# Attention by thirds of the queries: score products and value products in clusters, one exponential over two PSUM banks

## The chip, the cores and the metric

The kernel runs on one core of one Trainium2 chip. The metric is the device time of one execution in microseconds (us). Every execution was checked against the reference, and all of them were correct. With one core, an execution is called "slow" when it is over 1.5% above the fastest of the same kernel, otherwise "fast".

Engine names in the profile: PE is TensorE's matrix products, PEld its weight loads, DVE is VectorE, ACT is ScalarE, POOL is GpSimd, SP or SPq is the queue from which the transfers (DMA) are issued. L419 is line 419 of the kernel shown. Line numbers differ between kernels. SBUF and PSUM are the two on-chip memories in which the kernel allocates its tiles; in this kernel every product of TensorE goes to a PSUM tile.

## The reference, cut to what matters

The reference is attention with cluster routing (a query sees only the keys of its own cluster), followed by a mixture of small experts. There are 4 batches, 8 heads, 768 positions and a head size of 64.

```python
q_assign = argmax(q_n @ c_n.T); k_assign = argmax(k_n @ c_n.T)   # 16 clusters a head
scores = where(q_assign == k_assign, scale * q @ k.T, -1e9)
attn = softmax(scores)                  # over 768 keys
x = attn @ v                            # (4, 8, 768, 64) -> rows of 512
# then: gate of 8 experts, best 2, x + sum of w * (x @ A[e]) @ B[e]
```

## The kernel before: the parts that matter

The 32 heads are taken in 16 pairs. Each pair passes through these stages, several pairs at a time:

- Transposes of q and k, and the routing: logits, argmax, one-hot rows. The one-hot rows enter the score product as 16 more rows, so that the mask costs no step of its own.
- Scores with the keys on the partitions, and their exponentials ET. VectorE sums the exponentials into SS.
- Denominators: a product with ones on TensorE, a copy d_sb, four small transfers that spread the sums over 128 partitions (d_pk), a reciprocal r_pk, a transfer to DRAM (r_dr), and a broadcast from DRAM to all partitions (rDb).
- Value products into o, and a multiplication `xT = o * rDb` on VectorE.

The last two stages are what the argument is about. This is how they look before the change:

```python
def denominators(p):
    ...                                             # ones-product into ps
    nc.scalar.copy(d_sb[:], ps[:])
    for j in range(4):
        nc.sync.dma_start(d_pk[32*j:32*j+32, :], d_sb[32*j:32*j+1, :])
    def second():                                   # put into the program 3.2 us later
        nc.vector.reciprocal(r_pk[:], d_pk[:])
        r_dr = drp.tile([2, S], F32, name="r_dr")   # DRAM
        nc.sync.dma_start(r_dr[:].rearrange("h (i e) -> (h i) e", e=12), r_pk[:])
        rb = wk.tile([128, S], F32, name="rDb")
        for h in range(2):                          # two transfers, one for each head
            nc.sync.dma_start(rb[64*h:64*h+64, :], r_dr[h:h+1, :].to_broadcast([64, S]))
        rDb[p] = rb
    W.later(3.2, second)

def pv(p, c, kc):                                   # c: 512 or 256 queries, kc: key chunk
    for h in range(2):
        nc.tensor.matmul(ps[64*h:64*h+64, :], v_nat[p][:, h, kc*D:(kc+1)*D],
                         src[:, h, kc, :], start=(kc == 0), stop=(kc == T - 1))
...
    nc.vector.tensor_tensor(xT[p][:, a:b], O[p, c][:], rDb[p][:, a:b], ALU.mult)
```

A small scheduler decides the order of the program. It places the 18 score units of the next pair, one by one, between the value products of this pair.

The softmax here doesn't subtract the row's maximum and nothing guards it: scores larger than these inputs give would overflow.

Of the kernel before, what the change touches and what calls it, by code (L numbers as in the profile page):

```python
# [22 lines left out]
class Weave:  # L23
# [3 lines left out]
    def __init__(self):  # L27
        self.clock = 0.0
        self.heap = []
        self.n = 0  # L30

    def later(self, dt, fn):
        heapq.heappush(self.heap, (self.clock + dt, self.n, fn))
        self.n += 1

    def step(self, cost, fn):
        fn()
        self.clock += cost
        self.due()

    def due(self):
        while self.heap and self.heap[0][0] <= self.clock:
            heapq.heappop(self.heap)[2]()

    def flush(self):
        while self.heap:
            t, _, fn = heapq.heappop(self.heap)
            self.clock = max(self.clock, t)
            fn()

    def phase(self, events, fill):

        t0 = self.clock
        events = sorted(events, key=lambda e: e[0])
        fill = list(fill)
        while events or fill:
            if events and (events[0][0] <= self.clock - t0 or not fill):
                _, cost, fn = events.pop(0)
            else:
                cost, fn = fill.pop(0)  # L60
            self.step(cost, fn)
# [3 lines left out]
def kernel(  # L65
# [22 lines left out]
    C0, C1 = 512, 256  # L88
# [6 lines left out]
    etp = ctx.enter_context(tc.tile_pool(name="etp", bufs=2))  # L95
    wk = ctx.enter_context(tc.tile_pool(name="wk", bufs=1))
    wk2 = ctx.enter_context(tc.tile_pool(name="wk2", bufs=2))
    xp = ctx.enter_context(tc.tile_pool(name="xp", bufs=7))
# [4 lines left out]
    psc = ctx.enter_context(tc.tile_pool(name="psc", bufs=4, space=bass.MemoryType.PSUM))  # L103
# [3 lines left out]
    W = Weave()  # L107
# [7 lines left out]
    def load_qk(p):  # L115
        b, h = bh(p)
        t = nat.tile([128, 2, T, 2, D], F32, name="qk_nat")
        for w, x in ((0, q), (1, k)):
            for i in range(2):
                nc.sync.dma_start(t[:, w, :, i, :], x[b, h + i].rearrange("(p t) d -> p t d", t=T))  # L120
        qk_nat[p] = t

# [5 lines left out]

    load_qk(0)
# [78 lines left out]


    qkT = {}  # L210

    def turn(p, g):
        if g == 0:
            qkT[p] = wk.tile([128, 2 * S], F32, name="qkT")
        ps = psm.tile([128, 4, 128], F32, tag="m")
        src = qk_nat[p]
        for i in range(4):
            n = 4 * g + i
            w, t = divmod(n, T)
            nc.tensor.transpose(ps[:, i, :], src[:, w, t].rearrange("p h d -> p (h d)"), ident_f[:])  # L220
        dst = qkT[p][:, g * 512:(g + 1) * 512]
        if g == 1:
            nc.scalar.copy(dst, ps[:].rearrange("p i c -> p (i c)"))  # L223
        else:
            nc.vector.tensor_copy(dst, ps[:].rearrange("p i c -> p (i c)"))  # L225

    def rounded(p):
        x = qkT[p]
        qd, kd = Q2[p % 2], K2[p % 2]
        nc.gpsimd.tensor_copy(qd[0:64, 0, :].bitcast(F32R), x[0:64, 0:S])  # L230
        nc.gpsimd.tensor_copy(kd[0:64, 0, :].bitcast(F32R), x[0:64, S:2 * S])
        nc.gpsimd.tensor_copy(qd[:, 1, :].bitcast(F32R), x[:, 0:S])
        nc.vector.tensor_copy(kd[64:128, 1, :].bitcast(F32R), x[64:128, S:2 * S])
# [4 lines left out]
    def route(p):  # L238
        j = p % NP
        ps = psm.tile([128, 384], F32, tag="m")  # L240
# [6 lines left out]
        rt = wk2.tile([128, 384], F32, name="rt_sb")  # L247
        nc.scalar.copy(rt[:], ps[:])  # L248
        rt_sb[p] = rt

    def turn_logits(p):
        ps = psm.tile([128, 24, 16], F32, tag="m")
        for m in range(3):
            nc.tensor.transpose(ps[:].rearrange("p g c -> p (g c)")[:, m * 128:(m + 1) * 128],
                                rt_sb[p][:, m * 128:(m + 1) * 128], ident_f[:])
        mx = wk2.tile([128, 24], F32, name="mx")
        nc.vector.tensor_reduce(mx[:], ps[:], axis=AX.X, op=ALU.max)
        nc.vector.tensor_tensor(oh[p % 2][:, :, 0:16], ps[:],  # L258
                                mx[:].unsqueeze(2).to_broadcast([128, 24, 16]), ALU.is_equal)

    def turn_onehot(p):
        ps = psm.tile([128, T, 128], BF16, tag="m")
        v_ = oh[p % 2][:].rearrange("p (t g) c -> p t (g c)", g=4)
        for t in range(T):
            nc.tensor.transpose(ps[:, t, :], v_[:, t], ident_b[:])  # L265
        ohs = wk.tile([128, S], F32, name="ohs")
        nc.scalar.activation(ohs[:], ps[:].rearrange("p t c -> p (t c)"), ACTF.Copy,  # L267
                             scale=mscale[:, 0:1])
        qd, kd = Q2[p % 2], K2[p % 2]
        nc.sync.dma_start(qd[64:80, 0, :], ohs[0:16, :])  # L270
        nc.sync.dma_start(kd[64:80, 0, :], ohs[64:80, :])
        nc.sync.dma_start(qd[0:16, 1, :], ohs[32:48, :])
        nc.sync.dma_start(kd[0:16, 1, :], ohs[96:112, :])


    ET0, ET1, SS = {}, {}, {}

    def score_unit(p, u):
        if u == 0:
            ET0[p] = etp.tile([128, 2, T, C0], F32, name="ET0")  # L280
            ET1[p] = etp.tile([128, 2, T, C1], F32, name="ET1")
            SS[p] = wk2.tile([128, 2, S], F32, name="SS")
        qd, kd = Q2[p % 2], K2[p % 2]
        ps = psc.tile([128, 512], F32, name="sc")
        h = u % 2
        rows = 80 if h == 0 else 128
        if u < 12:
            kc = u // 2
            nc.tensor.matmul(ps[:], kd[0:rows, h, kc * 128:(kc + 1) * 128].bitcast(F32R),  # L289
                             qd[0:rows, h, 0:C0].bitcast(F32R))  # L290
            dst = ET0[p][:, h, kc, :]
        else:
            k2 = (u - 12) // 2
            for i in range(2):
                kc = 2 * k2 + i
                nc.tensor.matmul(ps[:, i * C1:(i + 1) * C1],  # L296
                                 kd[0:rows, h, kc * 128:(kc + 1) * 128].bitcast(F32R),
                                 qd[0:rows, h, C0:S].bitcast(F32R))
            dst = ET1[p][:, h, 2 * k2:2 * k2 + 2, :].rearrange("p a c -> p (a c)")
        nc.scalar.activation(dst, ps[:], ACTF.Exp, bias=expbias[:], scale=SCALE)  # L300
        W.later(1.3, lambda: add_unit(p, u))

    def add_unit(p, u):
        h = u % 2
        if u < 12:
            kc = u // 2
            E0, acc = ET0[p], SS[p][:, h, 0:C0]
            if kc == 1:
                nc.vector.tensor_tensor(acc, E0[:, h, 0, :], E0[:, h, 1, :], ALU.add)
            elif kc > 1:  # L310
                nc.vector.tensor_tensor(acc, acc, E0[:, h, kc, :], ALU.add)  # L311
        else:
            k2 = (u - 12) // 2
            E1, acc = ET1[p], SS[p][:, h, C0:S]
            if k2 == 0:
                nc.vector.tensor_tensor(acc, E1[:, h, 0, :], E1[:, h, 1, :], ALU.add)
            else:
                for i in range(2):
                    nc.vector.tensor_tensor(acc, acc, E1[:, h, 2 * k2 + i, :], ALU.add)  # L319
# [4 lines left out]
    def denominators(p):  # L324
        ps = psm.tile([128, 384], F32, tag="m")
# [4 lines left out]
        d_sb = wk.tile([128, 384], F32, name="d_sb")  # L330
        nc.scalar.copy(d_sb[:], ps[:])  # L331
        d_pk = wk2.tile([128, 12], F32, name="d_pk")
        for j in range(4):
            nc.sync.dma_start(d_pk[32 * j:32 * j + 32, :], d_sb[32 * j:32 * j + 1, :])  # L334

        def second():
            r_pk = wk2.tile([128, 12], F32, name="r_pk")
            nc.vector.reciprocal(r_pk[:], d_pk[:])  # L338
            r_dr = drp.tile([2, S], F32, name="r_dr")
            nc.sync.dma_start(r_dr[:].rearrange("h (i e) -> (h i) e", e=12), r_pk[:])  # L340
            rb = wk.tile([128, S], F32, name="rDb")
            for h in range(2):
                nc.sync.dma_start(rb[64 * h:64 * h + 64, :], r_dr[h:h + 1, :].to_broadcast([64, S]))
            rDb[p] = rb
        W.later(3.2, second)


    O = {}
    xT, xTb = {}, {}

    def pv(p, c, kc):
        n = (C0, C1)[c]
        if kc == 0:
            O[p, c] = pso.tile([128, n], F32, name=f"o{c}")
        ps = O[p, c]
        src = (ET0, ET1)[c][p]
        for h in range(2):
            nc.tensor.matmul(ps[64 * h:64 * h + 64, :], v_nat[p][:, h, kc * D:(kc + 1) * D],
                             src[:, h, kc, :], start=(kc == 0), stop=(kc == T - 1))
        if kc == T - 1:  # L360
            W.later(0.9, lambda: pv_out(p, c))

    def pv_out(p, c):
        if p not in rDb:
            W.later(0.4, lambda: pv_out(p, c))
            return
        if c == 0:
            xT[p] = xp.tile([128, S], F32, name="xT")
            xTb[p] = xbp.tile([128, S], BF16, name="xTb")
        a, b = ((0, C0), (C0, S))[c]  # L370
        nc.vector.tensor_tensor(xT[p][:, a:b], O[p, c][:], rDb[p][:, a:b], ALU.mult)  # L371
        nc.gpsimd.tensor_copy(xTb[p][:, a:b], xT[p][:, a:b])  # L372
# [4 lines left out]
    def gate(b):  # L377
        ps = psm.tile([128, 256], F32, tag="m")
# [5 lines left out]
        gl = mo.tile([96, 256], F32, name="gl")  # L384
        nc.scalar.copy(gl[:], ps[0:96, :])
        ms["gl"] = gl
# [113 lines left out]
    for i in range(2):  # L500
        zpart(b, i)
# [32 lines left out]
```

## Time and profile before

| | before |
|---|---|
| median of 3 executions (us) | 405.53 (404.97 to 406.09) |
| span of the profiled execution (us) | 400.8 |
| TensorE busy, VectorE busy, ScalarE busy | 91%, 67%, 58% |
| mean granted TensorE clock | 0.972 |
| a pair of heads (us) | 21.4 |

The first fence is the page's part on busy time, and from its 40 slices of the span the rows for TensorE (tenths busy) and for the TensorE clock that was granted (tenths of full speed).

```profile
span 400.8 us, 5985 instructions
PE 364.4 (91%) x2026; PEld 163.5 (41%) x2041; DVE 270.3 (67%) x548; ACT 232.2 (58%) x375; POOL 70.7 (18%) x92
...
PE   5437999999999999999999999999999999999645
...
PEclk9959999999999999999999999999999999999958
```

TensorE is at "9" from the fifth slice to the thirty-seventh, with the clock at nine tenths or more: it is the bound, and its order of work sets the time. The next fence is the timeline of TensorE before, in the middle of the run (start, duration, engine, line, operation, names, shapes, count).

```profile
209.30 1.08 PE L358 MATMUL o_1865<-ET_1650,v_nat 128*64 128x512 f32 x4
210.31 0.50 PE L289 MATMUL sc<-Q_0_152,K_0_154 128*128 128x512 f32 x1
210.64 0.60 PE L220 MATMUL ps<-ident_f,qk_nat 128*128 128x128 f32 x4
```

A single score product (L289) stands between other kinds of work. The numbers 128\*64 and 128\*128 are the tile of the array that a product takes. Each excursion from value products to one score product and back costs about 0.36 us beyond what the products themselves stream, by their start times. For example, two groups of four value records start at 186.72 and 188.16 us with one score product between them; at the spacing of long runs (0.21 us for 256 columns of values, 0.118 us for 256 of scores, so twice that here for 512) they would take 2 x 0.42 + 0.24 = 1.08 of these 1.44 us. This is what the change wants to save.

Two more views of before follow. The first is the list of waits of VectorE (who waited for whom: us in total, times, longest us), the second the list of transfer issues (KB each, median us from issue to landing).

```profile
DVE xT L371 <- DMA rDb<-r_dr: 47.1, 12, 5.7
```

```profile
rDb<-r_dr SPq DMA_DIRECT2D x32, 192.0 KB, 3.3
```

VectorE waits 47 us in total for the reciprocals' broadcast, while TensorE's own list of waits shows it waiting for the multiplication only once, for 5.5 us.

### The profile page before, as it was taken

Reading aid. Unit: us, or ns where it says so; the run is one execution under the profiler, and the core shown is the slowest. Engines: PE = TensorE matmul, PEld = TensorE weight load, DVE = VectorE, ACT = ScalarE, POOL = GpSimd, SP = SyncE. Lnnn points to the kernel's source line nnn. Section 1 sums busy time; section 2 is a strip of 40 time slices with the busy share of each in tenths; the row PEclk is TensorE's granted clock in tenths of the full one; section 3 lists DMA queues with packets and bytes.
Section 4 is the critical chain, followed back from the end, with each engine's and each line's share of the span. In section 5 each row is a group of like instructions: output and inputs, shape, how many; then the busy total and the mean of one; then the engine's idle time right before and its main releaser. Section 6 shows DMA issues by size and latency. Waiting matters only on the chain. (4 is left out here: it accounts for less than half of the span.)

```text
span 400.8 us, 5985 instructions
## 1 busy us (share of the span) xinstructions
PE 364.4 (91%) x2026; PEld 163.5 (41%) x2041; DVE 270.3 (67%) x548; ACT 232.2 (58%) x375; POOL 70.7 (18%) x92
## 2 busy tenths in 40 slices
PE   5437999999999999999999999999999999999645
PEld 2224343342424344454435353545443544433323
DVE  4237939668492979876586798875959797638043
ACT  1119766565646575757767676757676756663101
POOL 3202204012130401312131303030404030101000
PEclk9959999999999999999999999999999999999958
DMA  8726425160332416153626142363531211220204
GB/s 169 130 42 149 119 61 119 22 158 11 89 81 60 118 23 157 24 152 102 149 77 152 51 105 71 86 172 88 144 87 42 60 41 29 86 68 26 69 25 157
DMA packets 72974, 35.77 MB, mean 89 GB/s; under 512 B 62576, under 2 KB 66672, under 8 KB 72944
## 3 DMA queue, kind: packets, MB, share of 16 engines
q1 hardware_dynamic: 72944, 35.39, 35.4%
q8 instruction: 16, 0.26, 0.3%
q14 instruction: 14, 0.11, 0.1%
HBM read 25.74 MB, written 6.39 MB: 80 GB/s over the span
## 5 line engine op out<-in xcount | busy, mean ns | idle before, releaser
L372 POOL CAST xTb<-xT 128x512 bf16<-128x512 f32 (+1 forms) x32 | 23.9, 749 | 280.3 <-DVE xT L371 280.3
L289 PE MATMUL sc<-Q_0_152,K_0_154 80*128 80x512 f32 x96 | 43.4, 481 | 1.6 <-DMA K_0_154<-ohs 0.9
L289 PE MATMUL sc<-Q_1_153,K_1_155 80*128 80x512 f32 x96 | 42.1, 475 | 0.1
L220 PE MATMUL ps<-ident_f,qk_nat 128*128 128x128 f32 x192 | 31.6, 290 | 0.3
L289 PEld LDWEIGHTS sc<-Q_0_152,K_0_154 80*128 80x128 f32 x96 | 16.9, 188 | 32.2 <-issue 14.7
L220 PEld LDWEIGHTS ps<-ident_f,qk_nat 128*128 128x128 f32 x192 | 22.3, 146 | 18.2 <-DVE SS L311 4.9
L289 PEld LDWEIGHTS sc<-Q_1_153,K_1_155 80*128 80x128 f32 x96 | 16.7, 188 | 31.3 <-issue 18.2
L225 DVE COPY qkT<-ps 128x512 f32<-128x512 f32 x32 | 22.0, 687 | 7.1 <-PE ps L220 7.1
L329 PE MATMUL ps<-SS,ones 128*32 128x384 f32 x128 | 23.1, 498 | 3.3 <-DVE SS L319 2.6
L267 ACT ACTIVATE ohs<-ps,mscale 128x768 f32<-128x768 bf16 x16 | 14.4, 901 | 17.5 <-PE ps L265 17.5
L331 ACT COPY d_sb<-ps 128x384 f32<-128x384 f32 x16 | 7.7, 478 | 26.8 <-PE ps L329 18.1
L296 PE MATMUL sc<-Q_0_152,K_0_154 80*128 80x256 f32 (+1 forms) x96 | 22.2, 325 | 0.6 <-ACT ET_285 L300 0.6
L296 PE MATMUL sc<-Q_1_153,K_1_155 80*128 80x256 f32 (+1 forms) x96 | 21.9, 322 | 0.0
L338 DVE RECIPROCAL r_pk<-d_pk 128x12 f32<-128x12 f32 x16 | 3.7, 228 | 24.0 <-DMA d_pk<-d_sb 23.8
L296 PEld LDWEIGHTS sc<-Q_1_153,K_1_155 80*128 80x128 f32 (+1 forms) x96 | 13.9, 189 | 10.5 <-issue 4.6
L296 PEld LDWEIGHTS sc<-Q_0_152,K_0_154 80*128 80x128 f32 (+1 forms) x96 | 14.2, 189 | 9.7 <-issue 4.2
L223 ACT COPY qkT<-ps 128x512 f32<-128x512 f32 x16 | 9.4, 589 | 14.9 <-PE ps L220 12.9
L248 ACT COPY rt_sb<-ps 128x384 f32<-128x384 f32 x16 | 7.7, 479 | 16.9 <-PE ps L245 16.6
L245 PE MATMUL ps<-qkT,cnP 128*32 128x384 f32 x128 | 17.2, 498 | 0.2
L448 ACT COPY ot<-ps 128x512 f32<-128x512 f32 x12 | 7.0, 585 | 14.4 <-PE ps L444 8.2
L441 PE MATMUL ps<-ident_f,xT 128*128 128x128 f32 x96 | 14.9, 278 | 0.5 <-ACT ot L448 0.3
L265 PE MATMUL ps<-ident_b,oh_156 128*128 128x128 bf16 x48 | 4.4, 232 | 10.4 <-DVE oh_156 L258 10.4
(296 smaller groups left out, 790.3 us busy)
## 6 DMA issues: line engine op xcount, KB each, us to landing
qk_nat<-in_q_dram SPq DMA_DIRECT2D x32, 192.0 KB, 3.5
qk_nat<-in_k_dram SPq DMA_DIRECT2D x32, 192.0 KB, 4.1
v_nat<-in_v_dram SPq DMA_DIRECT2D x16, 384.0 KB, 4.3
rDb<-r_dr SPq DMA_DIRECT2D x32, 192.0 KB, 3.3
out_dram<-ot SPq DMA_DIRECT2D x24, 256.0 KB, 2.1
d_pk<-d_sb SPq DMA_DIRECT2D x64, 1.5 KB, 1.7
Q_0_152<-ohs SPq DMA_DIRECT2D x16, 48.0 KB, 2.1
K_0_154<-ohs SPq DMA_DIRECT2D x16, 48.0 KB, 2.1
```

Source lines behind the costliest of these rows:

```text
L220: nc.tensor.transpose(ps[:, i, :], src[:, w, t].rearrange("p h d -> p (h d)"), ident_f[:])
L223: nc.scalar.copy(dst, ps[:].rearrange("p i c -> p (i c)"))
L225: nc.vector.tensor_copy(dst, ps[:].rearrange("p i c -> p (i c)"))
L245: nc.tensor.matmul(ps[o:o + 32, :].rearrange("p (m c) -> p m c", m=3), cnP[:, j, :], xv[:, w, f])
L248: nc.scalar.copy(rt[:], ps[:])
L267: nc.scalar.activation(ohs[:], ps[:].rearrange("p t c -> p (t c)"), ACTF.Copy, scale=mscale[:, 0:1])
L289: nc.tensor.matmul(ps[:], kd[0:rows, h, kc * 128:(kc + 1) * 128].bitcast(F32R), qd[0:rows, h, 0:C0].bitcast(F32R))
L296: nc.tensor.matmul(ps[:, i * C1:(i + 1) * C1], kd[0:rows, h, kc * 128:(kc + 1) * 128].bitcast(F32R), qd[0:rows, h, C0:S].bitcast(F32R))
L329: nc.tensor.matmul(ps[o:o + 32, :], ones[:], SS[p][:, h, f * 384:(f + 1) * 384])
L331: nc.scalar.copy(d_sb[:], ps[:])
L372: nc.gpsimd.tensor_copy(xTb[p][:, a:b], xT[p][:, a:b])
L441: nc.tensor.matmul(ps[:, dc * 128:(dc + 1) * 128], xT[NP * b + dc][:, t * 128:(t + 1) * 128], ident_f[:], is_transpose=True, start=(dc == ...
```

## The change

The intent: take the queries of a pair in three thirds of 256. A slot for one third has eight score products of the next pair in a row, other work, four more score products, other work, and then the value products of this pair in a row (12 calls, which the trace shows as 24 records; below they are called 24 products). An exponential covers two PSUM banks (1,024 columns), so there are 9 a pair and not 18. A new scheduler keeps estimates of when each engine is done. The diff in its core, with cuts marked by `...`:

```diff
-    etp = ctx.enter_context(tc.tile_pool(name="etp", bufs=2))
+    etp = ctx.enter_context(tc.tile_pool(name="etp", bufs=4))
-    psc = ctx.enter_context(tc.tile_pool(name="psc", bufs=4, ... PSUM))
+    psc = ctx.enter_context(tc.tile_pool(name="psc", bufs=2, ... PSUM))   # two banks each
 ...
     def score_unit(p, t, u):
+        ps = psc.tile([128, 2, 2, TQ], F32, name="sc")
+        for i in range(2):
+            for h in range(2):
+                nc.tensor.matmul(ps[:, i, h, :], kd[...], qd[..., t*TQ:(t+1)*TQ])
+        W.op("ACT", 1.12, lambda: nc.scalar.activation(ET[p, t][:, 2*u:2*u+2]..., ps[:]..., ACTF.Exp, ...))
 ...                                 # adds over 1,024 columns: E0+E1, +E2, then the halves into SS
     def denominators(p):
 ...
-            for h in range(2):
-                nc.sync.dma_start(rb[64 * h:64 * h + 64, :], r_dr[h:h + 1, :].to_broadcast([64, S]))
-            rDb[p] = rb
+            def fill():
+                nc.sync.dma_start(rb[:], r_dr[:].unsqueeze(1).to_broadcast([2, 64, S]))
+                rDb[p] = rb
+            W.op("SP", 0.6, lambda: nc.sync.dma_start(r_dr[:]..., r_pk[:]),
+                 x, lag=1.6, then=lambda x: W.op("SP", 0.6, fill, x, key=("rDb", p), lag=3.4))
 ...
+    o4 = pso.tile([128, 4, TQ], F32)               # four thirds in two banks, one tile
     def pv(p, t):
+        i = NT * p + t
+        for kc in range(T):
             for h in range(2):
+                nc.tensor.matmul(o4[64 * h:64 * h + 64, i % 4, :], v_nat[p][...], ET[p, t][:, kc, h, :], ...)
 ...
+            nc.vector.tensor_tensor(xT[p][:, a:b], o4[:, i % 4], rDb[p][:, a:b], ALU.mult)
 ...
+    def slot(p, t):
+        if t == 0: ...; rounded(p + 2)             # three casts on GpSimd, one on VectorE
+        score_unit(p + 1, t, 0); score_unit(p + 1, t, 1)
+        for c in early: pe(*c)
+        score_unit(p + 1, t, 2)
+        for c in late: pe(*c)
+        pv(p, t)
```

Several transfers were also merged: q, k, and, in `fill`, the two broadcasts of the reciprocals into one.

## The prediction

> **What bounds the kernel now.** TensorE's order of work. The profile's first part gives TensorE 91% busy, VectorE 67%, ScalarE 58%; the slices show TensorE at "9" from about 50 to 365 us at full granted clock. Modelled ends hide gaps, so I read starts in the trace. A head pair takes 21.4 us (15 pairs between 42.6 us, the first value product, and 363 us, the last score product). Neighbours of a kind start 0.118 us (score products of 256 columns, also in a run of eight alternating heads) or 0.21 us apart (value products of 256). A round trip from values to one score product and back costs about 0.36 us beyond the streaming, and there are 218 runs of scores. The Trainium skill, "TensorEngine Tiling (Array Packing)", Key Properties, says that changing the tiling mode drains TensorE; values (128x64 tiles), denominators (128x32) and scores (full width) are different modes, and the 0.36 us agrees. Per pair, scores take 6.8 us and values 9.4 us.
>
> **What the change does**, per pair (three slots of eight score products, other work, four more, other work, 24 clustered value records):
> - Scores: 3 x (1.15 + 0.66) = 5.4 us, from runs of 8 and 4 in the trace.
> - Values: the one clustered group in the trace (pair 15, 256 columns) takes 2.69 us, so 8.0 us.
> - Other work unchanged: 3.5 us, and 1.6 us more with expert work.
> - Sum 16.9 us for four pairs, 18.5 us for eleven: 271 us instead of 320.
> - The third score unit waits for the first exponential: 1.12 us, extrapolated from 0.69 us at 512 columns with the copies' 0.85 ns a column. Costs 0.4 to 0.7 us a pair, 7 us.
> - ScalarE: 18 x 0.69 = 12.4 us becomes 9 x 1.12 = 10.1 us. Off the path.
> - VectorE: adds 3 x (1.20 + 1.20 + 0.68) = 9.2 us instead of about 11, but a 0.69 us copy more: 14.5 to 16 us of a pair of 17 to 19 us, nearly a second bound. It is in order, two PSUM buffers serve all other work, and the four value buffers share two banks, so the multiplication out of one half can hold up products into the other. I allow 0.8 us a pair, 12 us.
>
> Steady part about 290 us, 30 less. The start gets 2 us longer (one-hot rows come after two turns). The tail gets 6 us shorter: before, the last denominators wait behind adds and the reciprocals land 18.7 us after the last score product; that becomes about 13 us. In sum some 35 to 40 us less, nearly all of it on the critical path.
>
> **Predicted: 366 us, 8 in 10 between 353 and 382. Chances: faster by over 2% 0.96, within 2% 0.03, slower 0.01.**
>
> **What would show it.** Value clusters near 2.7 us, score clusters near 1.2 and 0.65 us; pairs of 17 to 20 us; TensorE with idle time before scores put down to ScalarE, before other work to VectorE; VectorE's share near 75%; ScalarE's busy time down by some 35 us; exponentials of 1.12 us; the last reciprocals some 13 us after the last score product.
>
> **What would make it wrong.** If VectorE, in order, is held by a late reciprocal transfer (it idled 47 us for these before, unharmed, by the list of waits), TensorE stops with it and the gain halves. If the multiplication and the products of one bank lock each other often, the same. If the schedule hides both, about 355 us.

## The result, and the profile after

The time went up. Ratios here and below are the mean time of one kernel's fast runs over that of the other's fast runs of the same rounds, so they are not quite the ratio of the medians quoted.

| | before | after |
|---|---|---|
| median (us) | 405.25 (4 executions, 404.36 to 406.09) | 506.53 (4 executions, 506.14 to 511.15) |
| ratio, 95% interval | | 1.2526 (1.2448 to 1.2603) |
| span of the profiled execution (us) | 400.8 | 504.5 |
| granted clock | 0.972 | 0.851 |
| a pair of heads (us) | 21.4 | 27.1 |

All these executions are fast. A pair of heads is the time from the first value product to the last score product, divided by 15, in both columns. Of the 104 us between the two spans, 85 us are lost between these two products, 8 us before them and 10 us after them. First the same parts of the page for after.

```profile
span 504.5 us, 6704 instructions
PE 360.3 (71%) x2617; PEld 229.9 (46%) x2617; DVE 267.6 (53%) x401; ACT 189.7 (38%) x218; POOL 92.1 (18%) x108
...
PE   6186939494958858397695939588595959875926
...
PEclk9679959697887978789797978879797988987978
```

TensorE now has holes: slices of 3 to 5 tenths stand beside slices of 9, and its clock falls to 7 tenths in slices among them. VectorE and ScalarE are less busy too, as a share. Nothing is saturated, so something makes everybody wait. The page's part on the chain of work that ended last names it (shares of the span, by engine and then by line; the second line is long, and is shown whole).

```profile
DMA 43%; PE 32%; DVE 11%; SPq 4%; ACT 4%; issue 3%; DVEq 0%; POOL 0%; ACTq 0%
DMA rDb<-r_dr 35%; PE o_183 L419 18%; PE sc L345 6%; DMA r_dr<-r_pk 4%; ACT ET L348 3%; DVE xT L431 2%; PE ps L381 2%; DMA d_pk<-d_sb 2%; SPq L392 1%; PE ps L258 1%; DVE mx L299 1%; DVE ACC L366 1%; PE ps L518 1%; DVE ACC L362 1%; DMA c_sb<-in_centroids_dram 1%
```

One transfer, the broadcast of the reciprocals, makes 35% of the chain. The lists of waits of after, first TensorE's longest, then VectorE's, say the same from the side of the engines.

```profile
PE o_183 L419 <- DVE xT L431: 96.7, 15, 8.6
```

```profile
DVE xT L431 <- DMA rDb<-r_dr: 95.1, 16, 9.4
```

Fifteen times, once for nearly every pair, TensorE stops before a value product until VectorE has done a multiplication, and VectorE stands still for the broadcast. In before the first line did not exist and the second was 47.1 us. The list of issues of after has the merged broadcast, without a landing time:

```profile
rDb<-r_dr SPq DMA_DIRECT2D x16, 384.0 KB
```

The landing can be read from the multiplication behind it: in all 16 pairs it starts 9.8 to 11.4 us after the issue has ended (median 10.3). By the same measure it is 2.8 to 4.0 us in before (median 3.1). The chain in order of time shows one whole turn of the loop in after (start us, duration us, what). Pieces named "issue" and others under 0.06 us are left out without a mark.

```profile
251.23 0.78 PE ps L381 x8
252.01 2.74 PE o_183 L419 x24
254.75 1.16 PE sc L345 x8
255.91 0.45 PE ps L258 x4
257.00 0.23 DVE r_pk L394
257.24 1.90 DMA r_dr<-r_pk
259.21 10.83 DMA rDb<-r_dr
270.07 0.77 DVE xT L431 x2
270.88 4.12 PE o_183 L419 x24
275.00 1.16 PE sc L345 x8
276.16 0.34 PE ps L294 x3
276.53 0.57 DVE mx L299
277.12 0.57 DVE oh_152 L300
277.83 0.85 PE ps L381 x8
```

The turn begins with the denominators of one pair (L381 at 251.23) and ends with those of the next (277.83): 26.6 us, of which the broadcast takes 10.83. The value products of the last third (L419 at 270.88) can't start before the multiplications at 270.07. The argmax (L299, L300) is behind the multiplication and the adds on VectorE, which works without a pause from 270.07 to 276.47; the chain names TensorE's transposed logits (L294), which end at the same time to within 0.03 us. The next denominators are behind the argmax. So the transfer is inside a cycle that every pair goes through once, and each microsecond of it is paid 16 times. The cluster after the stop takes 4.12 us where the same 24 products at 252.01 took 2.74: after such a stop the first products stand 0.42 us apart and not 0.21, which is another 1.4 us in this turn. The granted clock over the stretch 267.5 to 272.5 us is 0.50, and 1.00 over 251.9 to 264.6 and again over 275 to 277, so the doubled spacing falls together with the halved clock.

How the broadcast moves is visible in the records of its packets, each a row of 3,072 bytes. In before, 128 packets went in 1.9 to 2.4 us, with 16 to 19 packets of that size in flight at once. In after the 128 packets take some 9 us, each about 0.125 us. In two pairs of after no other packets of this size overlap, and there 2.0 are in flight on average: they run one behind the other in just two streams.

The rest of the change does what was intended. A value cluster takes 2.43 us from its first to its last start where it isn't stopped, which is so for 32 of the 48 (2.7 us with the last), eight scores about 1.2 us, four scores 0.72 to 0.83 us. The exponential over two banks takes 1.116 us, and ScalarE's busy time falls from 232.2 to 189.7 us.

### The profile page after: what moved, and what is told of

It reads as the page before. It is cut to its first block, busy times and chain, and to the rows that moved or that the text cites. A ratio compares the mean times of both kernels' runs of the same rounds, so it can differ in the third digit from the quotient of the medians.

```text
span 504.5 us, 6704 instructions
## 1 busy us (share of the span) xinstructions
PE 360.3 (71%) x2617; PEld 229.9 (46%) x2617; DVE 267.6 (53%) x401; ACT 189.7 (38%) x218; POOL 92.1 (18%) x108
## 4 chain that ended last, share of the span: by engine, by line
DMA 43%; PE 32%; DVE 11%; SPq 4%; ACT 4%; issue 3%; DVEq 0%; POOL 0%; ACTq 0%
DMA rDb<-r_dr 35%; PE o_183 L419 18%; PE sc L345 6%; DMA r_dr<-r_pk 4%; ACT ET L348 3%; DVE xT L431 2%; PE ps L381 2%; DMA d_pk<-d_sb 2%; SPq L392 1%; PE ps L258 1%; DVE mx L299 1%; DVE ACC L366 1%; PE ps L518 1%; DVE ACC L362 1%; DMA c_sb<-in_centroids_dram 1%
## 5 line engine op out<-in xcount | busy, mean ns | idle before, releaser
L348 ACT ACTIVATE ET<-sc,expbias 128x1024 f32<-128x1024 f32 x144 | 150.4, 1116 | 230.2 <-PE sc L345 230.2
L419 PE MATMUL o_183<-ET,v_nat 128*64 128x256 f32 x1152 | 164.6, 443 | 96.7 <-DVE xT L431 96.7
L419 PEld LDWEIGHTS o_183<-ET,v_nat 128*64 128x64 f32 x1152 | 90.4, 159 | 169.7 <-DVE xT L431 106.2
L434 POOL CAST xTb<-xT 128x256 bf16<-128x256 f32 x48 | 35.1, 751 | 330.5 <-DVE xT L431 330.5
L431 DVE TENSOR_TENSOR xT<-o_183,rDb 128x256 f32<-128x256 f32 x48 | 18.7, 420 | 112.2 <-DMA rDb<-r_dr 95.1
L362 DVE TENSOR_TENSOR ACC<-ET 128x1024 f32<-128x1024 f32 x48 | 61.0, 1270 | 9.5 <-ACT ET L348 9.4
L366 DVE TENSOR_TENSOR ACC<-ACC,ET 128x1024 f32<-128x1024 f32 x48 | 60.2, 1254 | 4.5
L345 PE MATMUL sc<-Q_0_148,K_0_150 80*128 80x256 f32 (+1 forms) x288 | 50.2, 310 | 4.9 <-ACT ET L348 3.5
L345 PE MATMUL sc<-Q_1_149,K_1_151 80*128 80x256 f32 (+1 forms) x288 | 47.8, 302 | 4.5 <-ACT ET L348 4.0
L345 PEld LDWEIGHTS sc<-Q_0_148,K_0_150 80*128 80x128 f32 (+1 forms) x288 | 39.5, 198 | 20.8 <-ACT ET L348 8.3
L345 PEld LDWEIGHTS sc<-Q_1_149,K_1_151 80*128 80x128 f32 (+1 forms) x288 | 37.8, 191 | 19.6 <-ACT ET L348 9.3
L367 DVE TENSOR_TENSOR SS<-ACC 128x512 f32<-128x512 f32 x48 | 38.0, 793 | 1.7
L258 PEld LDWEIGHTS ps<-ident_f,qk_nat 128*128 128x128 f32 x192 | 23.1, 145 | 11.5 <-issue 10.4
L381 PE MATMUL ps<-SS,ones 128*32 128x384 f32 x128 | 14.0, 508 | 6.9 <-DVE oh_152 L300 3.7
L266 POOL CAST K_1_151<-qkT 64x768 fp32r<-64x768 f32 x8 | 9.4, 1169 | 44.2 <-PE sc L345 30.2
L266 POOL CAST K_0_150<-qkT 64x768 fp32r<-64x768 f32 x8 | 13.3, 1667 | 20.1 <-DVE qkT L245 20.1
```

Of the source, the lines that this page charges most:

```text
L258: nc.tensor.transpose(ps[:, i, :], src[:, w, t].rearrange("p h d -> p (h d)"), ident_f[:])
L266: W.op("POOL", 1.0, lambda: nc.gpsimd.tensor_copy(kd[0:64, 0, :].bitcast(F32R), x[0:64, S:2 * S]), key=("r0", p))
L345: nc.tensor.matmul(ps[:, i, h, :], kd[0:rows, h, kc * 128:(kc + 1) * 128].bitcast(F32R), qd[0:rows, h, t * TQ:(t + 1) * TQ].bitcast(F32R))
L348: W.op("ACT", 1.12, lambda: nc.scalar.activation(ET[p, t][:, 2 * u:2 * u + 2].rearrange("p a h c -> p (a h c)"), ps[:].rearrange("p a h c ...
L362: nc.vector.tensor_tensor(f(acc[p, t][:]), f(E_[:, 0:2]), f(E_[:, 2:4]), ALU.add)
L366: nc.vector.tensor_tensor(f(a[:]), f(a[:]), f(E_[:, 4:6]), ALU.add)
```

## The experiments

My theory after reading the two traces: the merged broadcast alone makes the loss, because it lands some 7 us later and lies in a loop. Its rivals:

- The one tile o4 is to blame: the program makes products of a third wait for multiplications of other thirds, which a finer tile would avoid; with it, the late landing would be hidden.
- The schedule is to blame: it reckons with a landing after 3.4 us, and a better order would hide 10 us.
- VectorE is to blame as such: it has too much work, whatever the transfer does.

Three calls on three chips, and a fourth with one kernel. The medians of before in the same rounds were 404.6, 404.39, 403.74 and 403.81 us. (One execution of before took 1,769.81 us; it counts as slow and is left out of the ratios.)

### a1_two: after, with the two broadcasts of before

```diff
-                nc.sync.dma_start(rb[:], r_dr[:].unsqueeze(1).to_broadcast([2, 64, S]))
+                for h in range(2):
+                    nc.sync.dma_start(rb[64 * h:64 * h + 64, :], r_dr[h:h + 1, :].to_broadcast([64, S]))
```

> The changed kernel with one edit: the reciprocals are broadcast by two transfers of 64 partitions, as before the change, not by one of 128. Theory (a late transfer stops VectorE, and VectorE stops the last third's value products): in the changed kernel the transfer lands 10.3 us after its issue and TensorE waits 6 to 8 us a pair for the multiplication; with two transfers it lands in about 3.5 us, the wait falls under 1 us a pair, TensorE's clock stays up, and the time is 365 to 395 us. Rival (VectorE, or the two PSUM buffers, are overloaded by the clustered order): the transfer gets faster, but TensorE still waits several us a pair for VectorE; the time stays over 470 us.

Measured: 408.44 us median of four (402.51 to 411.30), of which two are slow; the two fast ones took 402.51 and 407.34 us, ratio to before 1.001 (0.9925 to 1.0095). One edit brings back nearly the whole loss of 101 us, but the time stays above the range that I had written down. The theory holds for the loss; it doesn't explain why the change gains nothing with the repair. That is a second question, taken up below.

### a2_split: after, with o4 split into two tiles

```diff
-    o4 = pso.tile([128, 4, TQ], F32)
+    oa = pso.tile([128, 2, TQ], F32, name="oa")       # thirds 0 and 1
+    ob = pso.tile([128, 1, TQ], F32, name="ob")       # third 2
-        if i > 3:
-            W.wait(("x", i - 4))
+        if p > 0:
+            W.wait(("x", i - 3))
+        o, sl = (oa, t) if t < 2 else (ob, 0)
```

> The changed kernel with one edit: the four value buffers, one tile of two banks, become two tiles of one bank: thirds 0 and 1 in one, third 2 in the other. The built program shows that third 2's products then wait for no multiplication. The single slow transfer stays. Theory: the wait of TensorE before third 2 goes (97 us in sum), but VectorE is still held by the transfer some 6 us a pair with adds and evacuations behind it, so TensorE stops later, for 2 to 4 us a pair: 415 to 470 us. If the lock of the shared tile alone were the cause: under 395 us. If the rival (overload) held: over 470 us.

Measured: 503.10 us, ratio 1.2453 (1.2384 to 1.2522). I had expected 415 to 470. The waits of the value products for the multiplication are nearly gone, as intended (96.7 us in after, 4.8 us here), and the time is the same. TensorE's list of waits shows where they went (a2_split):

```profile
PE sc L345 <- DMA Q<-ohs: 38.2, 11, 5.3
PE ps L381 <- DVE oh L300: 28.3, 8, 8.7
```

The stop moved from the value products to the next score products, whose one-hot rows are queued behind the slow broadcast, and to the denominators, which wait for the argmax behind the multiplication on VectorE. The shared tile is only the place where the loop closes first. As the sole cause of the loss it is ruled out.

### c2_rows_act: a2_split, with the one-hot rows issued from ScalarE's queue

```diff
-            nc.sync.dma_start(kd[64:80, 0, :], ohs[64:80, :])
+            nc.scalar.dma_start(kd[64:80, 0, :], ohs[64:80, :])
 ...                                                  # and the other three likewise
```

> The changed kernel with the split value tile (the run that missed its expectation at 503 us), plus: the four one-hot row transfers are issued from ScalarE's queue, not the queue that carries the slow broadcast. Theory (the split only moved the stop: the row transfers, issued 2 to 3 us after the broadcast in the same queue, land behind it, and the next pair's first scores need them; 38 us of waits in that run): the rows land in about 2 us again, TensorE's wait for them goes, and only VectorE's hold by the transfer stays: 430 to 485 us. Rival (the rows are late because the DMA engines are busy, whichever queue): within 2% of 503 us.

Measured: 518.63 us, ratio 1.2849 (1.2769 to 1.2929). Missed again, to the high side. The wait for the one-hot rows shrinks from 38.2 us in a2_split to 8.4. TensorE's list of waits of c2_rows_act now has the denominators first; the two lines name the two users of the small PSUM buffers that the argmax has to set free:

```profile
PE ps L381 <- DVE oh L300: 55.8, 8, 8.7
PE ps L520 <- DVE oh L300: 28.7, 4, 8.5
```

Twice I had opened the place where TensorE stood, and twice it stood at the next one. VectorE works in the order of the program, and its multiplication waits for the broadcast; the argmax, the adds and so the denominators are behind it. In one turn of c2_rows_act, VectorE works without a pause from the multiplication at 283.00 us to the end of the argmax at 290.58, and the denominators start at 290.73. This loop needs neither the shared tile nor the one-hot rows. Why c2_rows_act is another 3% slower than a2_split (ratios 1.2849 and 1.2453) stays open.

### a3_lag: after, with a schedule that knows the late landing

```diff
-  ... W.op("SP", 0.6, fill, x, key=("rDb", p), lag=3.4))
+  ... W.op("SP", 0.6, fill, x, key=("rDb", p), lag=10.4))
```

To build, it also needed a small mend of the scheduler (a list of waiting callbacks, instead of asking again every 0.3 us).

> The changed kernel with the schedule's estimate of the broadcast's landing set from 3.4 to 10.4 us (and the schedule's waiting list written so that this builds), so that the multiplications stand later in VectorE's order, behind third 2's products and adds. Same slow transfer, same single tile. Theory: the slow transfer harms only through the order; VectorE's wait for it falls from 95 us to under 30 us and the time is 370 to 405 us, a little over the run with two transfers because the last pair still waits 10 us for it. Rival (the transfer's load on the DMA engines or overload of VectorE costs the time): over 450 us.

Measured: 457.99 us, ratio 1.1336 (1.1263 to 1.1409), where I had expected 370 to 405; it lies in the range that I had given to the rival. VectorE's wait for the broadcast did fall as expected, from 95.1 to 8.7 us, so the order of VectorE's work hides about half of the loss. But a late landing has other followers than VectorE, so my reading that it harms only through the order was wrong. The rest stays: TensorE still waits for the multiplication (22.7 us in total) and for the one-hot rows (29.3 us) by its list of waits. The schedule's wrong estimate makes the slow transfer dearer, but it isn't the cause.

### b1_one: the kernel before, with nothing but the merged broadcast

```diff
-            for h in range(2):
-                nc.sync.dma_start(rb[64 * h:64 * h + 64, :], r_dr[h:h + 1, :].to_broadcast([64, S]))
+            nc.sync.dma_start(rb[:], r_dr[:].unsqueeze(1).to_broadcast([2, 64, S]))
```

> The kernel BEFORE the change with one line of the change: the reciprocals broadcast by one transfer of 128 partitions. Theory (that form of transfer is slow by itself): it lands in about 10 us here too, not 3.3, with no clustered order about; VectorE's wait for it rises from 47 us to over 100 us; the value buffers, single here, come free some 7 us later than the 18.5 of 21.4 us they now take, so TensorE stops about 3 to 4 us a pair: 440 to 480 us. Rival (the landing is slow only among the changed kernel's other transfers): 3 to 4 us landing, within 2% of before.

Measured: 505.57 us, ratio 1.2497 (1.2448 to 1.2545). This one line, in a kernel without clusters, thirds or the new scheduler, makes the whole loss, even more than I had expected. The longest wait in the list of VectorE and in that of TensorE, and two pieces of the chain in b1_one, which are the broadcasts of two neighbouring pairs:

```profile
DVE xT L370 <- DMA rDb<-r_dr: 159.3, 16, 13.4
PE o L357 <- DVE xT L370: 63.7, 15, 6.4
```

```profile
234.09 11.01 DMA rDb<-r_dr
...
261.50 11.04 DMA rDb<-r_dr
```

VectorE waits 159.3 us for the broadcast, against 47.1 in before, and TensorE waits 63.7 us before value products for the multiplication, which it never did in before. A turn takes 27.4 us (234.09 to 261.50), of which the broadcast takes 11.0. None of the three rivals can hold for this kernel: it has no o4, its order of work is that of before, and VectorE's work is unchanged too.

### b3_cols: the kernel before, with two broadcasts again, but cut by columns

After b1_one two readings were left: either it matters that it is one transfer and not two, or it matters what the pattern looks like. Here are two transfers, each with the pattern of the merged one.

```diff
-            for h in range(2):
-                nc.sync.dma_start(rb[64 * h:64 * h + 64, :], r_dr[h:h + 1, :].to_broadcast([64, S]))
+            for f in range(2):
+                nc.sync.dma_start(rb[:, f * 384:f * 384 + 384],
+                                  r_dr[:, f * 384:f * 384 + 384].unsqueeze(1).to_broadcast([2, 64, 384]))
```

> The kernel before, with the reciprocals still broadcast by two transfers, but cut by columns instead of by heads: each writes all 128 partitions for 384 of the 768 queries, so each has the broadcast pattern of two heads outermost. Two readings of what makes the merged transfer slow. First: the outermost size of two; the Trainium skill, DMA: Bandwidth & Descriptors, rules for kernel authors, confines such a transfer to at most two engines. Then both of these are slow as well: packets of 1536 bytes in two streams per transfer, the multiplication starts 6 to 11 us after the second issue, and the kernel takes 440 to 505 us. Second: that it is one transfer and not two, or the change of the schedule around it. Then this pair of transfers lands in 3 to 4 us like the pair by heads, and the kernel takes 400 to 410 us.

Measured: 510.89 us, ratio 1.2636 (1.2543 to 1.2729); a little over the range of the first reading and far from the second. The multiplication starts 9.7 to 10.9 us after the second issue has ended. VectorE's list of waits of b3_cols:

```profile
DVE xT L372 <- DMA rDb<-r_dr: 160.6, 16, 13.2
```

So two transfers can be as slow as one. Nor is one transfer of 384 KB over 128 partitions slow as such: the page of before has one, the load of v, whose pattern in the program has the 128 partitions outermost.

```profile
v_nat<-in_v_dram SPq DMA_DIRECT2D x16, 384.0 KB, 4.3
```

What the slow forms have in common, and the fast ones don't, is the outermost size of two. (They also share a repetition in the middle of the pattern; no run separates it from the size.) The Trainium skill, "DMA: Bandwidth & Descriptors", section "Why a DMA increments its semaphore by 16 and not by 1", says that a DMA is spread over the largest number of engines, up to 16, that divides the slowest dimension of each of its patterns, passing over dimensions of size one; and "Rules for kernel authors" says outright that "an outermost dim of size c < 16 — e.g. a leading zero-stride broadcast of c copies — confines the whole DMA to at most c engines". With c = 2 that is two engines; a transfer for one head, with 64 rows outermost, gets 16. The packets agree: two streams in after, and in b3_cols 256 packets of 1,536 bytes, 0.065 us each, in 9.0 us (median), which is again two at a time (256 x 0.065 / 2 = 8.3). That is two for both transfers together, where the expectation had two for each. An estimate from the page's two engines and the trace's 0.125 us a packet gives 64 x 0.125 = 8.0 us of packets for the merged form, and 8 x 0.125 = 1.0 us for 16 engines; the packets took 8.8 us in b1_one and 2.2 us in before (medians). The trace doesn't name the engine of a packet, so that there are two engines is the page's word; the runs show two streams.

There is no run with this broadcast as one fast transfer.

### a4_two_split: after, with both repairs, and the second question

> Both edits: two transfers, and the value buffers split over two tiles. Theory: if the fast transfer already removes the waits, the split adds little: within 3% of the run with two transfers alone, 360 to 390 us. If a remaining lock still costs, it is faster by over 3%.

The edit is that of a1_two and that of a2_split together. Measured: 401.35 us (400.71 to 402.11), ratio 0.9922 (0.9888 to 0.9957). I had expected 360 to 390. The split adds little to a1_two, as expected. With the broadcast quick and the tile split, some 35 us of the predicted gain are still missing. VectorE's wait for the broadcast in a4_two_split (95.1 us in after) and TensorE's longest wait, and then the groups by shape for two lines of VectorE (count, busy us, mean ns of one):

```profile
DVE xT L434 <- DMA rDb<-r_dr: 4.9, 5, 3.1
PE ps L381 <- DVE oh L300: 20.9, 9, 4.8
```

```profile
L367 DVE TENSOR_TENSOR SS<-ACC 128x512 f32<-128x512 f32 x48 | 38.0, 792 | 1.7
...
L269 DVE CAST K<-qkT 64x768 fp32r<-64x768 f32 x16 | 16.6, 1038 | 0.5
```

The denominators wait for a PSUM buffer that the argmax (L300) sets free. VectorE is late with it, since in the first third of a pair its work is longer than elsewhere: by the durations of the single instructions, 9 of the 48 adds of L367 take 1.19 to 1.20 us, where most take 0.69, and 7 of the 16 rounding casts of L269 take 1.50 to 1.51 us, where the shortest take 0.56. At that time GpSimd runs its three rounding casts: all nine long adds and all seven long casts overlap one of them in the trace. The Trainium skill, "SBUF — State Buffer", section "Who interferes with whom", says that a VectorE instruction with two inputs in SBUF contends with a GpSimd instruction that reads SBUF, and that casts on VectorE can contend too. Three runs test this.

### a5_round_t1: a4, with the rounding casts in the second third

```diff
-            if ok(p + 2):
-                rounded(p + 2)          # under: if t == 0
+        if t == 1 and ok(p + 2):
+            rounded(p + 2)
```

> The run with both repairs (two transfers, split value tile) plus: the rounding copies of the pair after next (three on GpSimd, one on VectorE) start at the second third of a pair, not the first. Theory: what is left over the predicted 366 us is VectorE's backlog at the first third, where an add takes 1.20 instead of 0.69 us and its rounding copy 1.50 instead of 0.56 us beside GpSimd's copies, so that the argmax comes late and the denominators wait 1.9 us a pair for its PSUM buffer. Moved, that wait falls from 21 us to under 6 us in sum: 375 to 390 us (from 401). Rival (the first third has too much work whatever GpSimd does, or too few PSUM buffers): over 396 us.

Measured: 376.30 us (375.92 to 376.73), ratio 0.9301 (0.9276 to 0.9327), as expected. TensorE's wait and the groups by shape of a5_round_t1:

```profile
PE ps L381 <- DVE oh L300: 7.2, 9, 2.1
L367 DVE TENSOR_TENSOR SS<-ACC 128x512 f32<-128x512 f32 x48 | 34.7, 722 | 1.7
...
L269 DVE CAST K<-qkT 64x768 fp32r<-64x768 f32 x16 | 8.9, 557 | 0.2
```

The mean add falls from 792 to 722 ns and the cast from 1,038 to 557 ns, and TensorE's wait for the argmax before the denominators falls from 20.9 to 7.2 us. The same work, moved by one third, is worth 25 us. The collision itself is not gone: of the 96 adds over 1,024 columns (L362, L366), 16 take over 1.5 us in a5_round_t1 and 5 in a4_two_split, where the median is about 1.23, and each of these overlaps a rounding cast of GpSimd. It has moved to where VectorE's delay costs less.

### a6_round_act: a4, with GpSimd's rounding casts on ScalarE

```diff
-        W.op("POOL", 1.0, lambda: nc.gpsimd.tensor_copy(kd[0:64, 0, :]..., x[0:64, S:2 * S]), key=("r0", p))
+        W.op("ACT", 0.82, lambda: nc.scalar.copy(kd[0:64, 0, :]..., x[0:64, S:2 * S]), W.clock + 3.2, key=("r0", p))
 ...                                     # the other two likewise
```

> The run with both repairs plus: GpSimd's three rounding copies are made by ScalarE, late in the first third; VectorE's rounding copy stays where it is. Theory (VectorE is slowed by GpSimd's copies beside it): the add falls from 1.20 to 0.7 us and VectorE's rounding copy from 1.50 to 0.6 us, the denominators' wait under 8 us in sum, ScalarE's busy time rises by about 40 us to 230 us without becoming a bound: 377 to 393 us. Rival (no slowing by GpSimd): the two durations stay, 400 us or more.

Measured: 384.20 us median of four (380.07 to 385.79; the highest is slow), ratio 0.9463 (0.9401 to 0.9524), as expected. Its profiled execution is slow; in it the add takes 696 ns and the cast 574 ns in the mean. The casts stayed in the first third here and only left GpSimd, so it is GpSimd that lengthens VectorE's work, and not the place in the slot. It gains less than a5: ScalarE's busy time goes up from 190.7 to 224.0 us, and TensorE waits 7.0 us for one-hot rows in this execution. How much of the difference each makes I did not separate.

### a7_t1_turn, a10_shared and a9_start: how far the clustered kernel goes

a7_t1_turn is a5 with one of a pair's three copies out of the transposes moved from VectorE to ScalarE:

```diff
-            e.append((0.44, lambda: turn(p + 3, t, "DVE"), ("nat", p + 3)))
+            e.append((0.44, lambda: turn(p + 3, t, "ACT" if t == 0 else "DVE"), ("nat", p + 3)))
```

> The run with both repairs and the moved rounding, plus: the first of the three evacuations of transposed queries and keys goes back to ScalarE, as one of three was before the change. Theory (VectorE's work in the first third is what TensorE waits for): 0.69 us a pair less on VectorE there; 2 to 8 us faster than the run with the moved rounding alone. If VectorE no longer bounds after the move: within 2 us of it.

Measured: 372.25 us (371.33 to 372.60), ratio 0.9195 (0.9163 to 0.9227): 4 us better than a5, as expected.

a10_shared is a7 with the one tile o4 back in place of oa and ob.

> The fastest run so far (372.3 us) with the value buffers again in one shared tile of two banks, as the change has them; two transfers, moved rounding and ScalarE's evacuation stay. Theory: with the reciprocals early, the shared tile costs little: third 0 of the next pair waits for the multiplication of third 2, 0.5 us a pair: 372 to 382 us. If the shared tile were harmful by itself: over 390 us.

Measured: 383.63 us, ratio 0.9493 (0.9442 to 0.9543), slightly over what I had expected. With a quick broadcast the shared tile costs 11 us (383.63 less 372.25). TensorE's waits of a10_shared show it, with 12.0 us at the very place that had 96.7 us in after:

```profile
PE o L420 <- DVE xT L432: 12.0, 10, 2.0
```

a9_start is a7 with the start of the kernel eased: the casts of the experts' weights go to GpSimd, and are placed two thirds of a pair later.

```diff
-        nc.vector.tensor_copy(b_b[:], b_f[:])
+        nc.gpsimd.tensor_copy(b_b[:], b_f[:])
 ...                                     # wgs and a_b likewise
-            if p == -2:
-                load_moe_weights()      # under: if t == 0
+        if p == -2 and t == 2:
+            load_moe_weights()
```

> The fastest run so far plus: the casts of the expert weights are made by GpSimd, after its first rounding copies, and the weights are loaded one third later, so that VectorE's first argmax does not stand behind their transfers (10 us of idle TensorE at the start, from 15.5 us on, in all kernels here). Expected: the first value product some 8 us earlier, 362 to 368 us. If another transfer then bounds the start: 370 us or more.

Measured: 366.16 us (366.11 to 368.15), ratio 0.9078 (0.9026 to 0.9130). The first value product starts at 43.26 us and no longer at 48.78, 5.5 us earlier where I had expected 8. This is the best version; it beats before by 9% and after by 28% (366.16 / 506.53). Its page:

```profile
PE 325.8 (89%) x2617; PEld 215.9 (59%) x2617; DVE 254.4 (70%) x379; ACT 197.3 (54%) x234; POOL 84.2 (23%) x114
...
PE   5748799999898998999999998999999999999955
```

TensorE is full again, with 325.8 us of busy time instead of the 364.4 of before. That is the gain of the clusters. In after itself it could not be seen: with a granted clock of 0.851 TensorE's busy time was 360.3 us there. I did not try a9_start's move of the experts' casts on the kernel before, where TensorE idles 10.4 us at the start too; without this move (a7_t1_turn) the ratio to before is 0.9195. The largest single group of waits of TensorE left is for exponentials, 8.8 us.

## Why the prediction was wrong, point by point

- **The bound before** was right: TensorE's order of work. The cost of the round trips was about right, too: a9_start has 39 us less busy time on TensorE than before (325.8 against 364.4), and takes 286 us from its first value product to its last score product, where about 290 was predicted and before took 320.5. This fits the page "TensorEngine Tiling (Array Packing)", Key Properties, that the prediction names; no run separates the drain that it speaks of from the rest of a round trip.
- **The sizes of the clusters and of the exponential** were right: 2.7 us predicted and measured for a value cluster, 1.15 and 0.66 predicted against 1.2 and 0.72 to 0.83 for the scores, 1.12 against 1.116 us for the exponential, 35 us less on ScalarE predicted against 42.5.
- **The step that failed** is "What the change does". It takes the score, value and other work, the adds and the copies, and leaves out the transfers. The diff merged the reciprocals' two broadcasts into one, and the sum has no term for this: it stands in it as zero. Measured, it is some 7 us a pair (10.3 us from issue to multiplication against 3.1), 16 times, in a loop with hardly any slack. Alone it makes 404 us into 506 (b1_one); taken out, it makes 507 into 405 (a1_two, mean of its fast executions).
- **The warning was there, its size was not.** "If VectorE, in order, is held by a late reciprocal transfer ... TensorE stops with it and the gain halves" is exactly the path that the chain of waits shows. But it was rated a remote case, with 0.01 for slower, since VectorE had idled 47 us for these transfers unharmed. I read that as slack. There was hardly any: in b1_one a landing some 7 us later cost (505.57 - 404.39) / 16 = 6.3 us a pair, so nearly all of it was passed on. That VectorE stood waiting for this very transfer in most pairs was the sign of it.
- **Why TensorE stops** needed three runs. I took the shared value tile, then the queue of the one-hot rows, for the way from VectorE to TensorE. a2_split and c2_rows_act opened these in turn and the time didn't fall, because VectorE's own order (multiplication, then adds and argmax, then denominators) closes the loop without them.
- **The allowance of 0.8 us a pair for VectorE**, 12 us in all, was too small. The collision of VectorE with GpSimd's casts in the first third alone is worth 17 to 25 us (a4 against a6 and a5), the shared tile 11 us (a10 against a7). The prediction had named the shared banks, but hadn't sized them, and hadn't thought of GpSimd at all.
- **The start and the tail.** I predicted 2 us more at the start. The first value product came at 50.7 us in after against 42.6 before, 8 us more; moving the experts' casts took back 5.5 us of the 6.2 that a7 still had (48.78 to 43.26). The tail, from the last score product to the last reciprocals, was to shrink from 18.7 to 13 us. To the first multiplication with these reciprocals it took 29.1 us in after, 10 of them in the broadcast, and 16.0 us in a9_start, so the predicted 13 was short even with the quick transfers.
- **The number 366 came out in the end** with a9_start, but that is not the predicted kernel: it has three repairs of after and two moves that the prediction knew nothing of. That it is the same number is chance; what the run shows is that the gain expected from the clusters was there and was covered up.

What stays open: how a9's remaining time divides, how a6 loses 8 us against a5, and why c2_rows_act is slower than a2_split. None of these touches the cause of the loss.

## What to carry to other kernels

When a diff merges two transfers into one, look at the outermost dimension of the new pattern before you count the saved issue: the bytes and the rows are the same, and still the landing can go from 3 to 10 us. An engine's wait that does no harm before a change is no slack by itself; find out whether the thing awaited lies in a loop from one iteration to the next, for there each added microsecond is paid once an iteration. And when you remove one wait and the time stays, the wait was a place and not a cause: follow the chain around until it comes back to where it began.

## What the Trainium skill lacked or had wrong

- "DMA: Bandwidth & Descriptors", "Rules for kernel authors": the row on two transfers to disjoint partition halves says not to bother and to use one transfer of 128 partitions. Here the two halves land about 3 us after their issue and the one transfer about 10 us, since its pattern has a size of two outermost. The row on using all 16 engines in the same table has the rule that decides; the first row should point to it.
- The same page gives a bandwidth of about 27 GiB/s per engine (29 bytes a nanosecond), but no measured example of a confined transfer. In these runs a stream moves a packet of 3,072 bytes in 0.125 us and one of 1,536 bytes in 0.065 us, about 24 bytes a nanosecond in both, and the packets of 384 KB over two streams took 8.8 us (median in b1_one).
- "SBUF — State Buffer", "Who interferes with whom": it names the contention without a size for adds of this shape. Here an add of 128x512 f32 with two SBUF inputs takes 1.20 us and not 0.69 while GpSimd casts run, and a rounding cast of 64x768 takes up to 1.51 us and not 0.56.
- "TensorEngine Tiling (Array Packing)", "Key Properties": the drain at a change of mode has no figure. Here the round trip from value products to a score product and back costs about 0.36 us, of which no run separates the drain.
